# A fused attention and feed-forward kernel: the first four tiles' q and k loaded in runs of 2 KB and turned by 64-row products, with the early order planned anew

## The chip, the cores and the metric

The kernel runs on one NeuronCore of a Trainium2 chip. The metric is device time in microseconds (us) of one execution; lower is better. Five engines work side by side, each through its own instructions in order: PE (TensorE, matrix products), DVE (VectorE), ACT (ScalarE), POOL (GpSimd) and SP, whose queue here only issues DMAs.

## The reference

```python
# q, k, v: 8 x 8 heads x 576 x 64, f32; w_in 512 x 2048 and w_out 2048 x 512, f64
q_c, k_c, v_c = (t.reshape(B, H, 9, 64, 64) for t in (q, k, v))     # chunks of 64 tokens
scores = matmul(q_c, k_c.transpose(0, 1, 2, 4, 3)) / 8
attn = exp(scores - max(scores)); attn = attn / (sum(attn) + 1e-9)
x = matmul(attn, v_c)  ->  4608 tokens x 512
h = x @ w_in
out = (max(h, 0) + log1p(exp(-abs(h)))) @ w_out
```

## The kernel before

A tile is 128 tokens (two chunks) with all 8 heads; there are 36. Four tiles make a block of 512 tokens, and a block goes through the two layers in 16 steps `fc`, each with 128 columns of `w_in` (G1, `gemm1`, L707, 12 products) and the matching 128 rows of `w_out` (G2, `gemm2`, L1076, 12 products). Each f32 operand is split into a high and a low part, so that three fast products stand for one exact one. The first two steps of the first block are cut: a0 and a1 are G1 of steps 0 and 1 for tiles 0 and 1 alone (12 products of 256 columns, L707), and their G2 (6 products of 512, L1076) follow; then come the same steps for tiles 2 and 3.

The weights are f64. Each of 32 units of 512 KB (16 of `w_in`, 16 of `w_out`, in turn) goes through one of three raw buffers: `w_load` (L314, L319, on SP), `w_top` (L327, ACT or POOL), `w_low` (L337, ACT), `w_add` (L342, DVE), `w_hi` (L364, ACT or POOL), `w_lo` (L368, DVE or POOL). A raw buffer is free again when its `w_top` and `w_low` are done. Tables (`TOP_ACT`, `HI_POOL`, `LO_POOL`) choose the engine.

Attention of tiles 0 to 3 is done in these steps for each tile i: loads of q, k, v (`pe_load`, L395); T, the turning of q and k from tokens on partitions to head dimensions on partitions (`pe_t`, L439); their copies out of PSUM, tq on ACT (L445) and tk on ACT or DVE (L449, table `TK`); S, the scores, 16 products of 64 x 64 (`pe_s`, L461); max (DVE, L620); sub, the subtraction of the maximum as one product (PE, L633); exp (ACT, L640); den, three DVE instructions (L645 to L647); norm (DVE or POOL, L652, table `NORM_POOL`); E, another turning (PE, L472); ec, its copy (ACT, L476); V, 16 products (PE, L487); xh (ACT, L680) and xl (DVE, L686), the two parts of x, which G1 reads. Behind a G1 stand softplus (ACT, L715), its high part (ACT, L719) and its low part (g_lo, DVE or POOL, L723), which G2 reads. Tiles 4 and on are turned on DVE instead (STREAM_TRANSPOSE, L547 and others) and their products stand between the G1 and G2 as bursts (L560, L665).

The order on every engine is fixed when the kernel is built. A planner (`Plan`) holds every step as a task with an engine, a cost, needs, buffers and an urgency `urg`. It plays the program through and gives each free engine the ready task with the lowest `urg`. Where it sees PE without work before 90 us it puts products of the identity there as fillers: `keep_warm` (L421) before many PE tasks, `keep_busy` (L416) before V of tile 2 and before a1. In the kernel before, the urgencies of the early tasks come from `ATT_AT`, `LOAD_AT`, `DECODE_AT` and formulas; the first loads on SP are q and k of tiles 0, 1, 3 and 2, one `w_in` unit, then the four v.

```python
    def pe_load(eng, i, src, n):                       # 1024 runs of 256 bytes
        dst = hd(slot(i, n))
        for p0, rows, b, s0 in rows_of(i):
            eng.dma_start(dst[p0 : p0 + rows], src[b, :, s0 : s0 + rows, :].rearrange("h s d -> s h d"))
    ...
                nc.tensor.transpose(                   # pe_t: four for q, four for k
                    dst[:, hp * P : (hp + 1) * P], src[:, 2 * hp : 2 * hp + 2, :], ident
                )
```

Of the kernel before, what the change touches and what calls it, by code (L numbers as in the profile page):

```python
# [192 lines left out]
def chunked_attention_softplus_ffn(  # L193
# [236 lines left out]
    def pe_t(i):  # L430
        if i < 2:
            tq, tk = (po_tile(n) for n in range(2))
        else:
            tq, tk = pa_tile(), pa_tile()
        keep_warm(tq)
        for dst, n in ((tq, 0), (tk, 1)):
            src = hd(slot(i, n))
            for hp in range(HP):
                nc.tensor.transpose(  # L439
                    dst[:, hp * P : (hp + 1) * P], src[:, 2 * hp : 2 * hp + 2, :], ident  # L440
                )
        live["t", i] = tq, tk

    def pe_tq(i):
        nc.scalar.copy(slot(i, 3), live["t", i][0])  # L445

    def pe_tk(i):
        copy = nc.scalar.copy if i not in TK else nc.vector.tensor_copy
        copy(slot(i, 4), live["t", i][1])  # L449

    def pe_s(i):
        qT, kT = (slot(i, n).rearrange("p (a t) -> p a t", a=HP) for n in (3, 4))
        sc = po_tile(2 + i % 2)
        keep_warm(sc)
        for hp in range(HP):
            for c2 in range(2):
                for h2 in range(2):
                    r = slice(h2 * C, (h2 + 1) * C)
                    t = slice(c2 * C, (c2 + 1) * C)
                    col = (2 * hp + c2) * C  # L460
                    nc.tensor.matmul(  # L461
                        sc[r, col : col + C], qT[r, hp, t], kT[r, hp, t], start=hp + c2 == 0, stop=True,
                        skip_group_check=True,
                    )
        live["sc", i] = [sc.rearrange("p (a c k) -> p a c k", c=2, k=C)]
        live["e", i] = slot(i, 0).rearrange("p (a c k) -> p a c k", c=2, k=C)
# [11 lines left out]
    def pe_v(i):  # L478
        eT, vt = slot(i, 1).rearrange("p (a t) -> p a t", a=HP), hd(slot(i, 2))
        xp = [pa_tile() for _ in range(2)]  # L480
        keep_busy() if i == 2 else keep_warm(xp[0])
        for hp in range(HP):
            for h2 in range(2):
                for c2 in range(2):
                    o = slice(((h2 + c2) % 2) * C, ((h2 + c2) % 2 + 1) * C)
                    r = slice(c2 * C, (c2 + 1) * C)
                    nc.tensor.matmul(  # L487
                        xp[c2][o, hp * C : (hp + 1) * C],
                        vt[r, 2 * hp + (h2 + c2) % 2, :],
                        eT[r, hp, o],  # L490
                        start=True,
                        stop=True,
                    )
        live["xp", i] = [t[:, : HP * C].rearrange("p (c a t) -> p c a t", c=1, t=C) for t in xp]

# [604 lines left out]
    def last_half(w, j):  # L1100
# [16 lines left out]
    T0 = 30.0  # L1117
    TG = 5.2
    DECODE_AT = (-20, -2.3, -8.9, -2, -60, 1.4, 0.2, -3, 2.1, -5, 5.9, 0)
    TK = (1, 2)  # L1120
    KS = 0.2
    ATT_AT = (-52.5, 101.4, -70.6, -226.8)
    LOAD_AT = (-104.1, -66.1, -54.8, -64.2, -28.7, -42.9, -41.8, -37.3, -47.5, -9.7, -24.4, -1.0, -1.7, 22.2)
    HI_POOL = (0, 1, 2, 3, 5, 6, 7, 8, 11, 12, 13, 15, 17, 18, 19, 20, 21, 25, 31)
    WHOLE = (4, 5, 9)
    SWAP_DVE = (4, 7, 9, 10, 11, 13, 14, 15, 16, 17, 19, 20, 21, 22, 23, 24, 25, 26, 27, 28, 29, 30, 31, 32, 33, 34, 35)
    SWAP_ACT = ()
# [24 lines left out]
        ("v", 10, 0, (0, 1)), ("v", 11, 0, (0, 1)), ("q", 13, 0, (2, 3)), ("k", 13, 0, (2, 3)),  # L1152
        ("v", 16, 1, (0, 1)), ("v", 17, 1, (0, 1)), ("v", 18, 1, (2, 3)), ("v", 19, 1, (2, 3)))})
    LOAD_POOL = ()
    TOP_ACT = (1, 4, 5, 6, 7, 8, 9, 12, 13, 14, 15, 17, 18, 19, 20, 22, 24, 25, 26, 28, 30)
    LOAD_AFTER = "q0"
    LO_POOL = (2, 3, 4, 7, 9, 11, 12, 13, 14, 17, 18, 19, 22, 23, 26, 29, 31)
    NORM_POOL = (0, 3, 4, 5, 6, 8, 11, 17, 20, 21, 28, 31, 29, 33)
    GLO_POOL = (0, 3, 6, 7, 8, 10, 13, 19, 22, 26, 28)
    WO_AFTER = 1.1  # L1160
    IN_SUPER = ((0, 0, 2), (0, 0, 5), (0, 0, 7), (0, 1, 5), (1, 0, 1), (1, 0, 3), (1, 0, 5), (1, 0, 7))
# [113 lines left out]
    for i in range(FIRST_BLK):  # L1275
        d, kw = ATT_AT[i], KS
        two = 2 * i // NCH != (2 * i + 1) // NCH
        for pl, (n, src) in enumerate((("q", q), ("k", k), ("v", v))):
            plan.add(f"{n}{i}", "SP", 0.6 * (1 + two), partial(pe_load, nc.sync, i, src, pl),
                     urg=LOAD_AT[i + 4 * (pl == 2)] + 0.1 * pl, kb=310, parts=1 + two,  # L1280
                     after=[f"q{i}"] if pl else [])
        plan.add(f"T{i}", "PE", 1.0, partial(pe_t, i), [f"q{i}", f"k{i}"], urg=d,
                 take=[("po0", [f"tq{i}"]), ("po1", [f"tk{i}"])] if i < 2 else [("pa", [f"tq{i}"]), ("pa", [f"tk{i}"])])
# [541 lines left out]
```

## Time and profile before

| | us |
|---|---|
| median of 3 runs | 810.44 (810.27 to 811.56) |
| the profiled execution, its own time | 809.8 |
| its span, first to last instruction | 808.0 |
| PE busy | 797.9 (99%) |
| DVE, ACT, POOL busy | 590.0, 425.2, 362.1 |

The profile records one execution. Its span is the time from the first to the last instruction; the execution's own time is 1.8 us longer. PE counts as busy also while it works on fillers.

### The profile page before, as it was taken

Reading aid. Unit: us, or ns where it says so; the run is one execution under the profiler, and the core shown is the slowest. Engines: PE = TensorE matmul, PEld = TensorE weight load, DVE = VectorE, ACT = ScalarE, POOL = GpSimd, SP = SyncE. Lnnn points to the kernel's source line nnn. Section 1 sums busy time; section 2 is a strip of 40 time slices with the busy share of each in tenths; the row PEclk is TensorE's granted clock in tenths of the full one; section 3 lists DMA queues with packets and bytes.
Section 4 is the critical chain, followed back from the end, with each engine's and each line's share of the span. In section 5 each row is a group of like instructions: output and inputs, shape, how many; then the busy total and the mean of one; then the engine's idle time right before and its main releaser. Section 6 shows DMA issues by size and latency. Waiting matters only on the chain.

```text
span 808.0 us, 15860 instructions
## 1 busy us (share of the span) xinstructions
PE 797.9 (99%) x5668; PEld 657.0 (81%) x5668; DVE 590.0 (73%) x1085; ACT 425.2 (53%) x719; POOL 362.1 (45%) x521
## 2 busy tenths in 40 slices
PE   8999999999999999999999999999999999999997
PEld 6878778888888888888888788888888888888886
DVE  4998996387287668868875888778889864334984
ACT  3757766254344555555455365655575444445451
POOL 1557647687888451124237664344102344110213
PEclk9999999999999999999999999999999999999999
DMA  9976658765675584898997755886537867666565
GB/s 216 254 206 198 176 180 218 235 187 166 148 225 117 155 252 169 258 278 228 280 258 229 236 125 156 236 204 186 159 122 223 282 195 221 191 192 201 162 220 144
DMA packets 192574, 163.34 MB, mean 202 GB/s; under 512 B 138288, under 2 KB 160048, under 8 KB 191600
## 3 DMA queue, kind: packets, MB, share of 16 engines
q1 hardware_dynamic: 168912, 97.56, 43.3%
q0 software_dynamic: 21472, 64.51, 26.9%
q8 instruction: 45, 0.74, 0.4%
q10 hardware_dynamic: 2112, 0.26, 0.2%
q14 instruction: 33, 0.27, 0.1%
HBM read 118.49 MB, written 42.47 MB: 199 GB/s over the span
## 4 chain that ended last, share of the span: by engine, by line
PE 88%; DVE 3%; DMA 3%; SPq 2%; ACT 1%; issue 1%; POOL 0%; ACTq 0%; POOLq 0%; DVEq 0%
PE pa L832 28%; PE po L1076 23%; PE po L1012 19%; PE pa L707 13%; PE pa L665 2%; DMA raw<-in_moe_w_in_dram 2%; SPq L395 2%; PE pa L560 2%; PE po L416 1%; DMA raw<-in_moe_w_out_dram 0%; DMA eT<-ka 0%; DVE ka L547 0%; DVE qe L547 0%; DVE g_lo L723 0%; DVE wib L342 0%
## 5 line engine op out<-in xcount | busy, mean ns | idle before, releaser
L801 POOL DMA_DIRECT2D xb<-scratch x79 | 43.2, 548 | 200.4 <-PE pa L832 154.5
L832 PE MATMUL pa<-wi_hi,xb 128*128 128x512 f32 x368 | 113.3, 389 | 0.0
L832 PE MATMUL pa<-wib,xb 128*128 128x512 f32 x432 | 105.0, 389 | 0.0
L832 PEld LDWEIGHTS pa<-wib,xb 128*128 128x128 f32 x432 | 81.1, 188 | 16.9
L1076 PE MATMUL po<-late,g_hi 128*128 128x512 f32 x300 | 90.9, 392 | 0.0
L846 DVE TENSOR_TENSOR wib<-wib,pa 128x512 f32<-128x512 f32 x72 | 49.4, 686 | 55.4 <-PE pa L832 47.6
L832 PEld LDWEIGHTS pa<-wi_hi,xb 128*128 128x128 f32 x368 | 69.1, 188 | 14.3
L1054 POOL DMA_DIRECT2D out_dram<-raw x56 | 36.3, 654 | 84.6 <-DVE raw L1041 83.2
L715 ACT ACTIVATE u<-pa 128x512 f32<-128x512 f32 (+1 forms) x50 | 29.0, 580 | 83.7 <-PE pa L707 83.5
L832 PE MATMUL pa<-wi_lo,xb 128*128 128x512 f32 x184 | 71.6, 389 | 0.0
L723 DVE TENSOR_TENSOR g_lo<-u,g_hi 128x512 fp32r<-128x512 f32 (+1 forms) x39 | 29.5, 755 | 54.1 <-ACT g_hi L719 53.8
L838 ACT COPY wib<-pa 128x512 f32<-128x512 f32 x72 | 41.7, 586 | 51.8 <-PE pa L832 51.6
L1076 PEld LDWEIGHTS po<-late,g_hi 128*128 128x128 f32 x300 | 55.8, 188 | 11.8
L1076 PE MATMUL po<-wo_hi,g_hi 128*128 128x512 f32 x160 | 59.6, 395 | 0.0
L1076 PE MATMUL po<-wo_hi,g_lo 128*128 128x512 f32 x160 | 59.0, 391 | 0.0
L1076 PE MATMUL po<-wo_lo,g_hi 128*128 128x512 f32 x160 | 58.8, 390 | 0.0
L1076 PE MATMUL po<-late,g_lo 128*128 128x512 f32 x160 | 58.4, 389 | 0.0
L707 PE MATMUL pa<-xb,wib 128*128 128x512 f32 x192 | 46.6, 390 | 0.8 <-DVE wib L368 0.5
L584 DVE STREAM_TRANSPOSE eT<-qe 32x256 f32<-32x256 f32 x104 | 45.1, 434 | 1.4
L1012 PE MATMUL po<-late,xb 128*128 128x512 f32 x180 | 43.9, 389 | 0.0
L707 PEld LDWEIGHTS pa<-xb,wib 128*128 128x128 f32 x192 | 35.8, 188 | 9.2 <-DVE wib L368 0.9
L832 PEld LDWEIGHTS pa<-wi_lo,xb 128*128 128x128 f32 x184 | 34.5, 188 | 7.3
(276 smaller groups left out, 1895.0 us busy)
## 6 DMA issues: line engine op xcount, KB each, us to landing
xb<-scratch POOLq DMA_DIRECT2D x48, 512.0 KB, 4.0
xb<-images SPq DMA_DIRECT2D x32, 512.0 KB, 4.7
raw<-in_moe_w_in_dram SPq DMA_DIRECT2D x16, 512.0 KB, 5.6
raw<-in_moe_w_out_dram SPq DMA_DIRECT2D x16, 512.0 KB, 4.5
scratch<-ends SPq DMA_DIRECT2D x16, 512.0 KB, 2.9
xb<-scratch POOLq DMA_DIRECT2D x7, 1024.0 KB, 6.6
xb<-scratch POOLq DMA_DIRECT2D x8, 768.0 KB, 7.5
late<-images SPq DMA_DIRECT2D x22, 256.0 KB, 4.2
```

What stands on the lines that cost most here:

```text
L395: eng.dma_start(dst[p0 : p0 + rows], src[b, :, s0 : s0 + rows, :].rearrange("h s d -> s h d"))
L584: nc.vector.transpose(live["eT", i][d : d + BL, tb], e[s : s + BL, kb])
L707: nc.tensor.matmul(ph, wt[:, c, :], x[:, ts_, c, :], start=(n == 0), stop=(n == 3 * KC - 1))
L715: nc.scalar.activation(w["u"], w["ph"], AF.Softplus)
L723: (nc.gpsimd if pool else nc.vector).tensor_tensor(w["lo"], w["u"], w["hi"].bitcast(F32), op=ALU.subtract)
L801: on("ring").dma_start(t[:, n * MT : (n + len(ks)) * MT], src[:, ks[0] * MT : (ks[-1] + 1) * MT])
L832: nc.tensor.matmul(w["bank"][BANK[k]], wts[:, q, c, :], x[:, c, :], start=k in OPENS and c + n == 0, stop=c == 1 and n == 2, skip_group_ch ...
L838: nc.scalar.copy(tmp_of(n), w["bank"][2 * (n == 2)])
L846: nc.vector.tensor_tensor(to, a, b, op=ALU.add)
L1012: nc.tensor.matmul(live["acc", ACC[k]][ct], image_part(n, k, j, q)[:, ct * P : (ct + 1) * P], g, start=k < 3 and j == 0 and i < len(cts), ...
L1054: eng.dma_start(out[r0 : r0 + MT, c0 : c0 + BL].rearrange("(b t) d -> t b d", t=BL), t.rearrange("t (b d) -> t b d", d=BL))
L1076: nc.tensor.matmul(pos[w["m"]][t], terms[n][0][:, j * P : (j + 1) * P], terms[n][1], start=(w["first"] and n == 0), stop=n == 2 and (w["la ...
```

## The change

q and k of tiles 0 to 3 are read as `h x (j d)`: head h and 16 groups x of 8 consecutive tokens j give the 128 partitions, and each partition holds 8 tokens of one head, 2 KB in one run. There are now 128 runs instead of 1024. v is loaded as before. A partition so holds (head, group), and a 512-wide row holds (token in the group, head dimension). T takes, for each of the 8 tokens j and each half a of the partitions (four heads), one 64 x 64 product with the identity: 16 products for q and 16 for k instead of four transposes of 128 x 128 each. The result has its columns in the order j, head, group, so tq and tk read PSUM with a stride (`in_order`) and write in order. S and V take their heads from other places; their products are as many and as large as before.

The rest is order. A table `START` gives new urgencies to all early tasks (some 300 of them, up to the last weight unit), and five tables move steps between engines: `TK` (tk on DVE: tiles 1 and 2 before, tile 3 now), `HI_POOL` (19 units before, 18 now), `TOP_ACT` (21 before, 19 now), `LO_POOL` (17 and 17), `NORM_POOL` (14 and 14).

```diff
     def pe_load(eng, i, src, n):
+        if n < 2:
+            (_, _, b, s0), = rows_of(i)
+            eng.dma_start(
+                slot(i, n), src[b, :, s0 : s0 + P, :].rearrange("h (x j) d -> h x (j d)", j=H)
+            )
+            return
         dst = hd(slot(i, n))
...
         for dst, n in ((tq, 0), (tk, 1)):
-            src = hd(slot(i, n))
-            for hp in range(HP):
-                nc.tensor.transpose(
-                    dst[:, hp * P : (hp + 1) * P], src[:, 2 * hp : 2 * hp + 2, :], ident
-                )
+            src = slot(i, n)
+            for j in range(H):
+                for a in range(2):
+                    r, col = slice(a * C, (a + 1) * C), slice(j * C, (j + 1) * C)
+                    nc.tensor.matmul(dst[r, col], src[r, col], ident[r, r], start=True, stop=True, skip_group_check=True)
...
+    def in_order(t):
+        return t.rearrange("p (j x) -> p x j", j=H)
+
     def pe_tq(i):
-        nc.scalar.copy(slot(i, 3), live["t", i][0])
+        nc.scalar.copy(slot(i, 3).rearrange("p (x j) -> p x j", j=H), in_order(live["t", i][0]))
...
+    START = dict(
+        q0=-55.2, k0=-55.15, q1=-42.45, k1=-42.6, q2=-55, T0=-51.9, k2=-42.55, tq0=63.85, tk0=59.32, S0=-51.9, w_top0=59.22,
...
-    TK = (1, 2)
+    TK = (3,)
...
+    for name, urg in START.items():
+        plan.tasks[name]["urg"] = urg
     plan.emit()
```

What the new order is, at three places. The first is PE at its start (`late0` and `late1` are q and k of tile 0, `late5` and `late6` those of tile 1, `xa` those of tile 3; `po` and `pa` are PSUM). Before:

```order
L439 MATMUL po0_150<-ident_92,late0_131 128x128 x4
L439 MATMUL po1_151<-ident_92,late1_132 128x128 x4
L421 MATMUL po2_179<-ident_92 128x128 x3
L461 MATMUL po2_179<-late4_135,late3_134 64x64 x16
L439 MATMUL po0_200<-ident_92,late5_138 128x128 x4
L439 MATMUL po1_201<-ident_92,late6_139 128x128 x4
L633 MATMUL po2_179<-mx_210,minus_97 128x512
```

And now:

```order
L447 MATMUL po0_152<-ident_92,late0_131 64x64 x16
L447 MATMUL po1_153<-ident_92,late1_132 64x64 x16
L447 MATMUL pa_196<-ident_92,xa_122 64x64 x16
L447 MATMUL pa_197<-ident_92,xa_122 64x64 x16
L470 MATMUL po2_236<-late4_135,late3_134 64x64 x16
L470 MATMUL po3_256<-ka_140,qe_139 64x64 x16
L639 MATMUL po2_236<-mx_275,minus_97 128x512
```

T of tile 3 now follows T of tile 0 at once, ahead of both S; behind the rows shown come sub of tile 3, T of tiles 2 and 1, S of both, E of tile 0, and sub of both.

The second place is PE around a0 and a1. Before, where a0 is ahead of the first row and the first G2 follows a1:

```order
L487 MATMUL pa<-xa,eT 64x64 x16
L416 MATMUL po_479<-ident 128x128 x10
L487 MATMUL pa<-late_169,late_170 64x64 x16
L416 MATMUL po_523<-ident 128x128 x12
L707 MATMUL pa<-xb,wi_hi 128x256 x4
L707 MATMUL pa<-xb,wi_lo 128x256 x4
```

And now:

```order
L497 MATMUL pa<-xa,eT 64x64 x16
L481 MATMUL po_509<-ident,late_230 128x128 x4
L497 MATMUL pa<-late_144,late_145 64x64 x16
L497 MATMUL pa<-late_231,late_232 64x64 x16
L427 MATMUL pa<-ident 128x128
L713 MATMUL pa<-xb,wi_hi 128x256 x4
L713 MATMUL pa<-xb,wi_lo 128x256 x4
L713 MATMUL pa<-xb,wi_hi 128x256 x8
```

All four V (tiles 0, 3, 2 and 1) stand ahead of a0, a1 follows a0 directly, and the 22 fillers of L416 are gone; behind a1 stand three fillers and then the first G2, that of a0.

The third place is DVE ahead of the low part of a0's softplus (the last row of each; `xb` is x, `wib` the weight units, `q` and `k` those of tile 4). Before:

```order
L686 TENSOR_TENSOR xb_354<-pa_379,xb_353 128x256
L686 TENSOR_TENSOR xb_354<-pa_380,xb_353 128x256
L547 STREAM_TRANSPOSE qe_442<-q_348 32x8x32 x4
L342 ISA wib1_103<-wib1_103,ends_124 128x1024
L368 TENSOR_TENSOR wi_lo_101<-wib0_102,wi_hi_100 128x512
L686 TENSOR_TENSOR xb_354<-pa_450,xb_353 128x256
L686 TENSOR_TENSOR xb_354<-pa_451,xb_353 128x256
L723 TENSOR_TENSOR g_lo_551<-u_468,g_hi_514 128x256
```

And now:

```order
L692 TENSOR_TENSOR xb_481<-pa_518,xb_480 128x256
L692 TENSOR_TENSOR xb_481<-pa_519,xb_480 128x256
L368 TENSOR_TENSOR wo_lo1_109<-wib1_103,wo_hi1_108 128x512
L342 ISA wib0_102<-wib0_102,ends_124 128x1024
L692 TENSOR_TENSOR xb_481<-pa_548,xb_480 128x256
L692 TENSOR_TENSOR xb_481<-pa_549,xb_480 128x256
L342 ISA wib1_103<-wib1_103,ends_124 128x1024
L553 STREAM_TRANSPOSE ka_599<-k_506 32x8x32 x4
L553 STREAM_TRANSPOSE qe_623<-q_450 32x8x32 x4
L729 TENSOR_TENSOR g_lo_632<-u_619,g_hi_629 128x256
```

In both, eight transposes of tile 4 stand ahead of that low part; now they follow xl of the last tile, with one more unit's sum (L342) ahead of them. Up to that low part DVE has six sums and three low parts of weights in the changed order, and four and two in the order before.

## Rows read from the trace of the kernel before

**Rows 1.** The page: the span, and busy time by engine.

```profile
span 808.0 us, 15860 instructions
PE 797.9 (99%) x5668; PEld 657.0 (81%) x5668; DVE 590.0 (73%) x1085; ACT 425.2 (53%) x719; POOL 362.1 (45%) x521
```

**Rows 2.** PE in order of time: start, us, line, xcount [idle before <-releaser].

```profile
26.77 0.69 PE L487 MATMUL pa<-xa,eT 64*64 64x64 f32 x32
27.39 2.50 PE L416 MATMUL po<-ident 128*128 128x128 f32 x20
...
30.45 2.94 PE L416 MATMUL po<-ident 128*128 128x128 f32 x24
33.15 0.72 PE L707 MATMUL pa<-xb,wi_hi 128*128 128x256 f32 x4
...
34.67 0.63 PE L1076 MATMUL po<-wo_hi,g_hi 128*128 128x512 f32 x2
```

**Rows 3.** The same view, the three waits of PE from 34 us to 798 us.

```profile
58.68 1.16 PE L707 MATMUL pa<-xb,wi_hi 128*128 128x512 f32 x4 [0.20 <-DVE qe L627]
...
83.67 2.97 PE L707 MATMUL pa<-xb,wib 128*128 128x512 f32 x12 [0.35 <-DVE qe L627]
...
112.50 2.11 PE L707 MATMUL pa<-xb,wib 128*128 128x512 f32 x8 [0.48 <-DVE wib L368]
```

**Rows 4.** The same view, PE up to 20 us.

```profile
1.35 3.60 PE L421 MATMUL po<-ident 128*128 128x128 f32 x16 [1.35 <-POOL ident masks.py:199]
4.79 1.15 PE L439 MATMUL po<-ident,late 128*128 128x128 f32 x8
...
12.94 1.02 PE L633 MATMUL po<-mx,minus 128*128 128x512 f32 x2
13.97 1.15 PE L461 MATMUL po<-late,late 64*64 64x64 f32 x32
15.05 0.66 PE L472 MATMUL po<-ident,late 128*128 128x128 f32 x4
...
19.18 0.69 PE L487 MATMUL pa<-late,late 64*64 64x64 f32 x32 [1.33 <-DMA late<-in_v_dram]
```

**Rows 5.** DMA, 5 to 11 us: packets; then GB/s from 0 to 45 us in 40 slices.

```profile
DMA packets 5214, 1.31 MB, mean 219 GB/s; under 512 B 5214, under 2 KB 5214, under 8 KB 5214
...
GB/s 0 45 257 234 227 221 217 218 218 223 279 324 231 221 165 229 243 343 358 379 290 165 101 290 321 231 305 294 327 156 319 296 224 26 211 254 117 375 200 167
```

**Rows 6.** DVE in order of time.

```profile
16.05 0.68 DVE L645 TENSOR_REDUCE den<-late 128x8 f32<-128x512 f32 x1
...
17.09 0.64 DVE L620 TENSOR_REDUCE mx<-po 128x8 f32<-128x512 f32 x1
...
23.22 2.14 DVE L342 CUSTOM_DVE_ANT_0 wib<-wib,ends 128x1024 uint16<-128x1024 uint16 x2
...
27.74 0.69 DVE L342 CUSTOM_DVE_ANT_0 wib<-wib,ends 128x1024 uint16<-128x1024 uint16 x1
28.35 0.68 DVE L368 TENSOR_TENSOR wi_lo<-wib,wi_hi 128x512 fp32r<-128x512 f32 x1
29.05 1.79 DVE L547 STREAM_TRANSPOSE qe<-q 32x256 f32<-32x256 f32 x4
30.87 1.42 DVE L686 TENSOR_TENSOR xb<-pa,xb 128x256 fp32r<-128x256 f32 x4
32.21 0.41 DVE L723 TENSOR_TENSOR g_lo<-u,g_hi 128x256 fp32r<-128x256 f32 x1
```

**Rows 7.** ACT in order of time.

```profile
10.80 0.58 ACT L449 COPY ka<-pa 128x512 f32<-128x512 f32 x1
...
23.23 0.79 ACT L327 CAST ends<-raw 128x512 f16<-128x512 bf16 x1 [0.61 <-DMA raw<-in_moe_w_in_dram]
```

**Rows 8.** POOL in order of time.

```profile
11.68 1.04 POOL L652 TENSOR_TENSOR late<-late,den 128x512 f32<-128x512 f32 x1 [9.76 <-DVE den L647]
```

More of the change, by code (lines that the diff above doesn't have):

```diff
@@ L436, in pe_t @@
         for dst, n in ((tq, 0), (tk, 1)):
-            src = hd(slot(i, n))
-            for hp in range(HP):
-                nc.tensor.transpose(
-                    dst[:, hp * P : (hp + 1) * P], src[:, 2 * hp : 2 * hp + 2, :], ident
-                )
+            src = slot(i, n)
[3 more added lines that the diff above has]
+                    nc.tensor.matmul(dst[r, col], src[r, col], ident[r, r], start=True, stop=True, skip_group_check=True)
         live["t", i] = tq, tk
+    def in_order(t):
+        return t.rearrange("p (j x) -> p x j", j=H)
     def pe_tq(i):
-        nc.scalar.copy(slot(i, 3), live["t", i][0])
+        nc.scalar.copy(slot(i, 3).rearrange("p (x j) -> p x j", j=H), in_order(live["t", i][0]))
     def pe_tk(i):
         copy = nc.scalar.copy if i not in TK else nc.vector.tensor_copy
-        copy(slot(i, 4), live["t", i][1])
+        copy(slot(i, 4).rearrange("p (x j) -> p x j", j=H), in_order(live["t", i][1]))
     def pe_s(i):
-        qT, kT = (slot(i, n).rearrange("p (a t) -> p a t", a=HP) for n in (3, 4))
+        qT, kT = (slot(i, n).rearrange("p (h t) -> p h t", h=HP) for n in (3, 4))
         sc = po_tile(2 + i % 2)
         keep_warm(sc)
-        for hp in range(HP):
+        for hl in range(HP):
             for c2 in range(2):
-                for h2 in range(2):
-                    r = slice(h2 * C, (h2 + 1) * C)
+                for a in range(2):
+                    r = slice(a * C, (a + 1) * C)
                     t = slice(c2 * C, (c2 + 1) * C)
-                    col = (2 * hp + c2) * C
+                    col = (2 * hl + c2) * C
                     nc.tensor.matmul(
-                        sc[r, col : col + C], qT[r, hp, t], kT[r, hp, t], start=hp + c2 == 0, stop=True,
+                        sc[r, col : col + C], qT[r, hl, t], kT[r, hl, t], start=hl + c2 == 0, stop=True,
                         skip_group_check=True,
@@ L482, in pe_v @@
         for hp in range(HP):
-            for h2 in range(2):
+            for n in range(2):
                 for c2 in range(2):
-                    o = slice(((h2 + c2) % 2) * C, ((h2 + c2) % 2 + 1) * C)
-                    r = slice(c2 * C, (c2 + 1) * C)
+                    h2 = (n + c2) % 2
+                    h = 2 * hp + h2
+                    o, r, t = (slice(m * C, (m + 1) * C) for m in (h2, c2, h // HP))
                     nc.tensor.matmul(
[L488 to L492, printed above, removed]
+                        xp[c2][o, hp * C : (hp + 1) * C], vt[r, h, :], eT[r, h % HP, t], start=True, stop=True
                     )
@@ L1123, in chunked_attention_softplus_ffn @@
     LOAD_AT = (-104.1, -66.1, -54.8, -64.2, -28.7, -42.9, -41.8, -37.3, -47.5, -9.7, -24.4, -1.0, -1.7, 22.2)
-    HI_POOL = (0, 1, 2, 3, 5, 6, 7, 8, 11, 12, 13, 15, 17, 18, 19, 20, 21, 25, 31)
+    HI_POOL = (0, 1, 2, 4, 5, 6, 10, 11, 12, 13, 15, 17, 18, 19, 20, 21, 25, 31)
     WHOLE = (4, 5, 9)
@@ L1154, in chunked_attention_softplus_ffn @@
     LOAD_POOL = ()
-    TOP_ACT = (1, 4, 5, 6, 7, 8, 9, 12, 13, 14, 15, 17, 18, 19, 20, 22, 24, 25, 26, 28, 30)
+    TOP_ACT = (1, 2, 6, 8, 9, 12, 13, 14, 15, 17, 18, 19, 20, 22, 24, 25, 26, 28, 30)
     LOAD_AFTER = "q0"
-    LO_POOL = (2, 3, 4, 7, 9, 11, 12, 13, 14, 17, 18, 19, 22, 23, 26, 29, 31)
-    NORM_POOL = (0, 3, 4, 5, 6, 8, 11, 17, 20, 21, 28, 31, 29, 33)
+    LO_POOL = (2, 3, 6, 8, 10, 11, 12, 13, 14, 17, 18, 19, 22, 23, 26, 29, 31)
+    NORM_POOL = (2, 3, 4, 5, 6, 8, 11, 17, 20, 21, 28, 29, 31, 33)
     GLO_POOL = (0, 3, 6, 7, 8, 10, 13, 19, 22, 26, 28)
@@ L1279, in chunked_attention_softplus_ffn @@
             plan.add(f"{n}{i}", "SP", 0.6 * (1 + two), partial(pe_load, nc.sync, i, src, pl),
-                     urg=LOAD_AT[i + 4 * (pl == 2)] + 0.1 * pl, kb=310, parts=1 + two,
+                     urg=LOAD_AT[i + 4 * (pl == 2)] + 0.1 * pl, kb=310 if pl == 2 else 230, parts=1 + two,
                      after=[f"q{i}"] if pl else [])
```

34 lines of the change are left out of this document (added).

## The prediction

> **What bounds the kernel now.** I read the page first: PE is busy for 797.9 us of a span of 808.0 [rows 1]. Fillers count as busy there, so the question is from when on PE's work is all useful and unbroken. PE in order of time answers it: 44 filler products stand between 27.4 and 33.4 us, a1 starts at 33.15, and the first product of the second layer (the first G2, that of a0) at 34.67 [rows 2]. From there to 800 us the same view has three waits of PE, 0.20, 0.35 and 0.48 us, each ended by DVE [rows 3]. So the end of the kernel is the start of that first G2, plus a fixed list of products, plus 1.03 us of waits. A change of the early part can pay in two ways only: the first G2 starts earlier, or those waits go. Nothing beyond 1.03 us can come from weights that are ready sooner.
>
> **The loads.** Eight loads of 256 KB go from 1024 runs of 256 bytes to 128 runs of 2 KB. While runs of 256 bytes alone were moved, all were under 512 bytes and the rate was 219 GB/s; the best slices with long runs show 343 to 379 GB/s [rows 5]. A load so falls from 1.20 us (262 KB by 219) to about 0.71 (by 370), eight of them by 3.9 us. Both ends: nothing, if the run length isn't what limits, and 4.0 us at 379. On the path it is worth little. The fillers held PE until T of tile 0 began at 4.79 [rows 4]; one filler of eight goes, 1/8 of 3.60, so T can start at about 4.3. After that PE is the later one, as the next part shows. The weights behind these loads do come some 4 us sooner, which helps the waits of [rows 3].
>
> **The turning.** T was 8 transposes in 1.15 us, and the next PE work followed after about 1.1 [rows 4]. It becomes 32 products of 64 x 64 in two of the array's four quarters (rows and columns are cut by the same half). The nearest rows are S, 16 such products in the same two quarters: it starts at 13.97 and the next at 15.05, so 1.08 us [rows 4]. T so takes 2.15. Ends: V runs 16 products of that size over all four quarters in 0.69 [rows 4], so 1.4 for T is the low end, the old 1.1 the lowest; twice the 1.15 that S shows, 2.3, the high one. I take 2.15, since S has T's shape and its quarters. Four tiles: 4 x 1.05 = 4.2 us more PE work ahead of the first G2. The Trainium skill (TensorEngine Tiling (Array Packing), Restrictions and Gotchas) speaks against this change: with the columns cut, the transpose mode for f32 isn't to be had. No run here shows the rule itself; that S, by ordinary products, has twice as many PE records as calls, and the transposes one each, fits it. With the transposes' old price kept, the sum below would be 4.2 us less.
>
> **tq and tk.** Their copies read PSUM with a stride. A plain copy takes 0.58; a strided cast on ACT 0.79 [rows 7]. I take 0.58, the same shape and type, and keep 0.2 more for each, of which two stand on the path.
>
> **The new order, step by step** (us from the span's start; each step begins where its last input or its engine is free). T of tiles 0 and 3: 4.3 to 8.6. S of both: 10.8. sub of both, 1.0 each [rows 4]: 12.8. T of tiles 2 and 1: 17.1. S of tile 2: 18.2. S of tile 1 waits for two copies behind the last T, 0.55 each: 18.3 to 19.4. E of tile 0, 0.6 [rows 4], and sub of tile 2: 21.05. exp of tile 2, 0.6: 21.7. den, 1.04 for its three instructions from 16.05 to 17.09 [rows 6]: 22.8. norm of tile 2 is on POOL, 1.04 [rows 8]: 23.9. E of tile 2, V of tile 3, E of tile 1 and V of tile 2, 0.6 each on PE: 26.4. xh of tile 2, behind the copy of tile 1's E on ACT: 27.3. From here DVE is full: xl of tile 2, 0.7; a low part, 0.68; a sum, 0.65; xl of tile 1, 0.7; a sum, 0.65; eight transposes of tile 4, twice 1.79; g_lo, 0.41 [rows 6]: 27.3 + 7.4 = 34.7. a0 and a1 are done by about 32, and PE then has little. With 0.2 from DVE to PE the first G2 starts at **34.9**, against 34.67. No v is late in this: all loads up to the last v are 5.2 MB, by about 20 us at the rates above, ahead of its V.
>
> So the fillers that go (2.50 and 2.94 us) and the loads bring nothing: dearer turns and a DVE queue take their place. What DVE has gained is work: at its g_lo of a0 it has two sums and a low part more behind it than before, and one tk copy less to do. That is 1.9 us ahead, and the first two of the three waits of [rows 3] were at products that waited for DVE's subtractions, the third for a low part of a weight on DVE. I let 0.20 and 0.48 go and keep 0.35, whose burst is ordered much as before.
>
> **What moves between engines.** Two w_top from ACT to POOL, one w_hi from POOL to ACT, one tk from DVE to ACT: POOL has 0.9 us more, ACT 0.4 less, DVE 0.7 less. I cost these at nothing: POOL is busy for 45% [rows 1]. If that cover is gone, it shows on DVE, where two sums beside POOL's work took 2.14 us [rows 6] instead of 1.3.
>
> **The sum.** +0.2 for the first G2, -0.7 for the waits: -0.5. Against the profiled execution's 809.8 that is 809.3; the median of the runs shown stands 0.6 above it, so **809.9**. Ends: the first G2 4.2 us earlier with all waits gone gives 805.4; 0.4 for the copies, two hits of 0.85 on DVE and no wait gone give 812.7. A measurement of this kernel can tell about 0.2%, 1.6 us, from no change.
>
> **Rival 1, turns that cost little: faster.** Everything up to the last V hangs on PE, so a cheaper T goes through whole. At the transposes' price the time is 809.9 - 4.2 = 805.7; half way, 807.8. For it: V shows that 64 x 64 products can run at 0.69 for 16. Against it: V uses four quarters, T two. The Trainium skill (TensorEngine Tiling (Array Packing), Tiling Modes) counts four such tiles that work independently; by that the price of V would hold only for products over all four, and the rows of S and V agree. A shorter DVE queue ahead of g_lo would do the same in part. It decides from a first G2 ahead of 33.8. I give it 0.32.
>
> **Rival 2, DVE held up by POOL: slower.** Place: DVE from 20 to 35 us. There are eight DVE instructions of weights and norm ahead of g_lo, and POOL now has more of the same. In the row of 23.22 POOL's norm ran beside two sums, and they took 0.85 longer [rows 6]. Two such hits, the dearer copies (0.4) and no wait gone: 809.9 + 1.7 + 0.4 + 0.7 = 812.7. For it: in the new order g_lo is the last of a full queue, so each hit goes through whole. Against it: xl waits for ACT in between, which takes up the first. It decides from a first G2 behind 36.5. I give it 0.15.
>
> **Rival 3, the clock: slower.** With 22 filler calls gone, PE idles for most of the time from 32 to 34.9. The first fillers took 0.225 each, at the lower clock of 1.2 GHz; the later ones 2.50 for 20, so 0.125, at 2.4 [rows 2, 4]. The clock rose by about 4.8 us, some 3.4 us after PE's first product [rows 4]. If it falls in the gap, PE works at half rate for as long again and loses 1.7: 811.6. Against it: a wait of 1.33 us with thin work around it left the products behind it at their full rate [rows 4]. The Trainium skill (TensorE: Matmul & The Clock Gate, HAM oscillation) names gaps between groups of products as what throttles the clock again, and a busy start as what pays once more; no row before shows it in mid-run. I give it 0.07.
>
> **How the numbers follow.** The forecast has 0.46; its own range is 808.9 to 812.0, the part of the ends that a measurement can't tell from no change. Faster by over 0.2% is rival 1: 0.32. Slower is rivals 2 and 3: 0.22. The range reaches down to 806.2, between rival 1's two times, and up to 812.2, between those of rivals 2 and 3; about 1 in 10 is left out at each side.
>
> **What would show it.** T as 64 records in 2.1 us, with the next PE work right behind; T of the last tile ending near 17; the q and k loads' issues on SP at about half their time; the first G2 at 34 to 36, with the g_lo of a0 right ahead of it on DVE behind eight transposes; PE's waits behind it under 0.7 us in sum; the granted clock at full throughout. I am wrong in size if T takes 1.1 to 1.5 or the first G2 is at 33 or earlier, in sign if it is behind 36.5, and in mechanism if PE's waits behind it grow.

## The result, and the profile after

The changed kernel takes 815.88 us (median of 6 runs, 815.47 to 817.5) against 810.71 (6 runs, 810.12 to 811.72): 1.0067 times as long, 95% interval 1.0054 to 1.008. It is slower by 5.2 us where no change was forecast, outside the range. The profiled execution took 815.57 us, its span is 813.8, 5.8 more than before.

The page of the changed kernel (as [rows 1]):

```profile
span 813.8 us, 16206 instructions
PE 800.0 (98%) x5846; PEld 659.5 (81%) x5846; DVE 588.3 (72%) x1084; ACT 424.7 (52%) x719; POOL 362.5 (45%) x522
```

PE of the changed kernel in order of time (start, us, line, xcount, [idle before <-releaser]), as [rows 2 to 4]. L447 is T, L470 S, L497 V, L713 a0 and a1, L1082 the first G2:

```profile
4.82 1.15 PE L447 MATMUL po<-ident,late 64*64 64x64 f32 x32
6.40 1.15 PE L447 MATMUL po<-ident,late 64*64 64x64 f32 x32 [0.44 <-DMA late<-in_k_dram]
7.78 1.15 PE L447 MATMUL pa<-ident,xa 64*64 64x64 f32 x32 [0.23 <-DMA xa<-in_q_dram]
9.41 1.15 PE L447 MATMUL pa<-ident,xa 64*64 64x64 f32 x32 [0.49 <-DMA xa<-in_k_dram]
10.39 1.10 PE L470 MATMUL po<-late,late 64*64 64x64 f32 x32
...
16.30 1.15 PE L447 MATMUL pa<-ident,late 64*64 64x64 f32 x32 [0.71 <-DMA late<-in_k_dram]
18.71 3.50 PE L447 MATMUL po<-ident,late 64*64 64x64 f32 x64 [1.27 <-DMA late<-in_q_dram]
22.04 1.11 PE L470 MATMUL po<-late,late 64*64 64x64 f32 x32
...
35.36 1.09 PE L713 MATMUL pa<-xb,wi_hi 128*128 128x256 f32 x4 [0.32 <-ACT xb L686]
...
40.41 0.71 PE L1082 MATMUL po<-wo_hi,g_hi 128*128 128x512 f32 x2
...
41.43 0.62 PE L1082 MATMUL po<-wo_hi,g_lo 128*128 128x512 f32 x2
...
117.39 2.12 PE L713 MATMUL pa<-xb,wib 128*128 128x512 f32 x8 [0.60 <-DVE wib L368]
```

Half a turn costs 0.98 us where work follows at once (9.41 to 10.39), within 0.1 of the forecast. But PE waits for q and k five times, 3.14 us in sum, where before the list of its waits has none for them; and T of tile 1 takes 3.50 for 64 records. The first G2 starts at 40.41 instead of 34.67: 5.74 us, the whole loss. Two waits follow it, 0.60 and 0.21, against three of 1.03 in sum.

DVE of the changed kernel, the low part of a0 (g_lo):

```profile
40.52 0.42 DVE L729 TENSOR_TENSOR g_lo<-u,g_hi 128x256 fp32r<-128x256 f32 x1
```

The same kernel by stretches (us, busy time and instructions of each engine, granted clock, DMA share, GB/s), and behind it the first stretch of the kernel before:

```profile
2.50:6.50 4.00, 3.45 (x45) 3.02 (x45) 0.00 (x0) 0.00 (x0) 0.00 (x0) 1.00 0.50 169
18.50:22.00 3.50, 3.29 (x64) 3.32 (x65) 0.59 (x1) 0.07 (x1) 0.05 (x1) 0.52 0.95 285
35.50:39.00 3.50, 3.50 (x18) 3.50 (x18) 3.44 (x9) 2.98 (x5) 2.40 (x3) 0.51 0.93 285
```

```profile
2.50:6.50 4.00, 4.00 (x27) 3.78 (x25) 0.00 (x0) 1.08 (x2) 0.00 (x0) 1.00 1.28 240
```

While almost only runs of 2 KB are moved, the DMA share is 0.50 and the rate is 169 GB/s instead of 240: longer runs, and slower. And the granted clock is 0.52 and 0.51, the lower level of 1.2 GHz, under T of tile 1 and under a0 and a1; in the kernel before the clock's row has 1.00 throughout. PE had idled several times ahead of both.

SP of the changed kernel in order of time (DMA issues: start, us):

```profile
2.24 0.60 SPq L395 DMA_DIRECT2D xa<-in_q_dram  x1
...
4.66 2.02 SPq L314 DMA_DIRECT2D raw<-in_moe_w_in_dram  x1
6.72 1.39 SPq L395 DMA_DIRECT2D late<-in_k_dram  x1
...
9.41 1.64 SPq L395 DMA_DIRECT2D late<-in_k_dram  x1
```

An issue is down to 0.60, but the four from 4.66 on take 1.2 to 2.0 us; no run here shows what holds SP. The last k is issued at 9.41; before, all eight were out by 8.5.

### The profile page after: what moved, and what is told of

Read it like the earlier page. It is cut to its first block, busy times and chain, and to the rows that moved or that the text cites. A ratio compares the mean times of both kernels' runs of the same rounds, so it can differ in the third digit from the quotient of the medians.

```text
span 813.8 us, 16206 instructions
## 1 busy us (share of the span) xinstructions
PE 800.0 (98%) x5846; PEld 659.5 (81%) x5846; DVE 588.3 (72%) x1084; ACT 424.7 (52%) x719; POOL 362.5 (45%) x522
## 4 chain that ended last, share of the span: by engine, by line
PE 87%; DMA 4%; POOL 2%; DVE 2%; ACT 2%; issue 1%; SPq 1%; DVEq 0%; POOLq 0%; ACTq 0%
PE pa L838 27%; PE po L1082 21%; PE po L1018 19%; PE pa L713 15%; PE pa L671 2%; PE pa L566 2%; DMA late<-in_q_dram 1%; DMA xb<-scratch 1%; POOL raw L536 1%; DMA k<-in_k_dram 1%; SPq L395 1%; DMA raw<-in_k_dram 1%; PE po L447 0%; DMA raw<-in_moe_w_out_dram 0%; DVE eT L602 0%
## 5 line engine op out<-in xcount | busy, mean ns | idle before, releaser
L1082 PE MATMUL po<-late,g_hi 128*128 128x512 f32 x300 | 91.2, 392 | 0.0
L1082 PEld LDWEIGHTS po<-late,g_hi 128*128 128x128 f32 x300 | 55.8, 188 | 12.2 <-DVE late L368 0.4
L1082 PE MATMUL po<-wo_hi,g_hi 128*128 128x512 f32 x160 | 59.7, 395 | 0.0
L1082 PE MATMUL po<-wo_hi,g_lo 128*128 128x512 f32 x160 | 59.0, 391 | 0.0
L1082 PE MATMUL po<-wo_lo,g_hi 128*128 128x512 f32 x160 | 58.8, 390 | 0.0
L1082 PE MATMUL po<-late,g_lo 128*128 128x512 f32 x160 | 58.4, 389 | 0.0
L713 PE MATMUL pa<-xb,wib 128*128 128x512 f32 x192 | 46.4, 390 | 0.6 <-DVE wib L368 0.6
L713 PEld LDWEIGHTS pa<-xb,wib 128*128 128x128 f32 x192 | 36.0, 188 | 8.5 <-DVE wib L368 1.0
```

Of the source, the lines that this page charges most:

```text
L713: nc.tensor.matmul(ph, wt[:, c, :], x[:, ts_, c, :], start=(n == 0), stop=(n == 3 * KC - 1))
L1082: nc.tensor.matmul(pos[w["m"]][t], terms[n][0][:, j * P : (j + 1) * P], terms[n][1], start=(w["first"] and n == 0), stop=n == 2 and (w["la ...
```

## The experiments

The Trainium skill (DMA: Bandwidth & Descriptors, How many engines (k)) says that a DMA from a hardware queue is spread over the largest number of engines, 16 at most, that divides the slowest dimension of both access patterns. The changed loads have heads, 8, as the slowest dimension of the source. That rule gave theory A. Times in the table are in us, "first G2" is its start, and "records" are those that PE shows for one product of T. All times below are medians beside runs of the kernel before on the same chip (810.3 to 810.6; 810.71 beside the change).

| run | loads | turning | order | us | ratio (95%) | first G2 |
|---|---|---|---|---|---|---|
| change | heads first | two records | new | 815.88 | 1.0067 (1.0054 to 1.008) | 40.41 |
| e1 | groups first | two records | new | 816.72 | 1.0079 (1.0066 to 1.0092) | 40.20 |
| e6 | heads first | one record | new | 816.83 | 1.0077 (1.0065 to 1.0089) | 38.23 |
| e5 | groups first | one record | new | 811.11 | 1.0006 (0.9996 to 1.0016) | 34.38 |
| e3 | as before | as before | new | 811.09 | 1.0013 (1.0001 to 1.0024) | 34.86 |
| e2 | heads first | two records | old | 816.87 | 1.0079 (1.0063 to 1.0095) | 38.79 |
| e7 | groups first | two records | old | 816.91 | 1.0074 (1.0061 to 1.0087) | 41.39 |
| e8 | groups first | one record | old | 811.83 | 1.0024 (1.0008 to 1.004) | 36.07 |

### Which part costs: e1 to e4

**e1_groups_first**

```diff
-                slot(i, n), src[b, :, s0 : s0 + P, :].rearrange("h (x j) d -> h x (j d)", j=H)
+                slot(i, n), src[b, :, s0 : s0 + P, :].rearrange("h (x j) d -> x h (j d)", j=H)
```

> The changed kernel with one line other: each q and k load walks the group of eight tokens first and the head second, so the same 128 runs of 2 KB of a load go to other partitions, with a slowest dimension of 16 instead of 8. Nothing else moves. This changes the computation: a partition holds another head and group than the turning takes it for, so times alone count. Theory A (a load with a slowest dimension of 8 is moved by half of the DMA engines, and the first G2 is late because q and k are): the DMA share from 2.5 to 6.5 us goes from 0.50 to about 1, PE's five waits for q and k (3.1 us in sum) go, the fall of the clock at 18.5 us goes too; first G2 at 36 to 37.5 us instead of 40.4; 811 to 813 us. Theory B (runs of 2 KB are no faster whatever walks them, or PE's dearer turns and the new order set the time): the share stays near 0.5 and the time at 815 to 816.5; or the loads land sooner and the first G2 still stands behind 39.5.

816.72 us. The stretch from 2.5 to 6.5 us:

```profile
2.50:6.50 4.00, 4.00 (x45) 3.78 (x45) 0.00 (x0) 0.00 (x0) 0.00 (x0) 1.00 1.02 268
```

PE of the same run:

```profile
1.35 3.35 PE L427 MATMUL po<-ident 128*128 128x128 f32 x14 [1.35 <-POOL ident masks.py:199]
4.63 3.40 PE L447 MATMUL po<-ident,late 64*64 64x64 f32 x64
7.87 2.03 PE L447 MATMUL pa<-ident,xa 64*64 64x64 f32 x64
9.74 1.10 PE L470 MATMUL po<-late,late 64*64 64x64 f32 x32
10.79 1.15 PE L470 MATMUL po<-ka,qe 64*64 64x64 f32 x32
11.87 1.98 PE L639 MATMUL po<-mx,minus 128*128 128x512 f32 x4
13.78 0.56 PE L447 MATMUL pa<-ident,late 64*64 64x64 f32 x12
15.72 1.67 PE L447 MATMUL pa<-ident,late 64*64 64x64 f32 x51 [1.37 <-issue]
...
19.16 0.45 PE L470 MATMUL po<-late,late 64*64 64x64 f32 x10
22.75 1.78 PE L470 MATMUL po<-late,late 64*64 64x64 f32 x53 [3.15 <-issue]
...
40.20 0.71 PE L1082 MATMUL po<-wo_hi,g_hi 128*128 128x512 f32 x2
...
473.30 0.69 PE L566 MATMUL pa<-ka,qe 64*64 64x64 f32 x32 [1.68 <-DVE ka L543]
```

The first half of theory A is shown: one dimension moved doubles the DMA share, the rate goes from 169 to 268 GB/s and all five waits for q and k are gone. So the Trainium skill's rule agrees with the row. The second half fell: not a microsecond was won. In the middle of T of tile 2 and of S of tile 2 PE stands still for 1.37 and 3.15 us, and "issue" says that nothing in the profile ended these waits. They eat up all that the loads gained. The last row is a wait of which the change has 0.21; most of the 1.6 us by which this run ends later than its first G2 alone would make it.

**e2_loads_alone**: the kernel before with the changed `pe_load`, `pe_t`, `pe_tq`, `pe_tk`, `pe_s` and `pe_v`, and nothing else.

> The kernel before with the changed loads, turning, copies, S and V alone: its tables, its urgencies, so its order on every engine and its fillers. Theory A (the loads on half of the engines and the dearer turns make it slower, whatever the order): PE waits for q and k here too; the first G2 is at 37.5 to 40 us instead of 34.7; 813.5 to 816 us. Theory B (the new order is what costs, the loads and turns are hidden): first G2 at 34.7 to 36, 810.5 to 812.

816.87 us, just above theory A's range. PE of that run:

```profile
17.17 1.15 PE L447 MATMUL pa<-ident,late 64*64 64x64 f32 x32 [0.54 <-DMA late<-in_k_dram]
...
38.79 0.63 PE L1082 MATMUL po<-wo_hi,g_hi 128*128 128x512 f32 x2
```

The first G2 is 4.12 us later. The forecast's price for four turns was 4 x 1.05 = 4.2, and here, with the 44 fillers, the granted clock is 1.00 throughout. From each T to PE's next work, waits left out, the four T take 8.8 us against 4.2 before, 4.6 more: the term is right. That the first G2 comes so close to it is in part luck: PE starts T of tile 0 0.27 later and waits 0.54 for a k, and the wait of 1.33 for v [rows 4] is gone. The remaining 1.9 us of the profiled execution come later, in single waits (0.7 for a softplus's high part on ACT).

**e3_order_alone**: the changed kernel with the functions of `pe_load`, `pe_t`, `pe_tq`, `pe_tk`, `pe_s` and `pe_v` from the kernel before.

> The changed kernel with the loads, turning, copies, S and V of the kernel before: runs of 256 bytes, eight transposes for a tile; the new urgencies and tables, so the new order on every engine. Theory A (the order is as good as the old one or better; loads and turns cost the time): first G2 at 33 to 36 us, 808.5 to 811.5. Theory B (the order costs by itself, by its DVE queue, or by PE idling where the 22 fillers stood, so that the clock falls): first G2 behind 37, 813 to 816, with a fall of the clock in the early part.

811.09 us. PE of that run:

```profile
16.32 1.08 PE L439 MATMUL po<-ident,late 128*128 128x128 f32 x4 [1.38 <-DMA late<-in_k_dram]
...
34.86 0.73 PE L1076 MATMUL po<-wo_hi,g_hi 128*128 128x512 f32 x2
...
36.78 0.73 PE L1076 MATMUL po<-wo_hi,g_lo 128*128 128x512 f32 x2 [0.72 <-DVE g_lo L723]
```

The order costs next to nothing by itself (1.0013): theory A. Yet PE waits five times for q and k here too, 3.13 us in sum, as much as in the change: in the new order PE is ahead of the old loads as well. What is left of the loss, over 4 us, belongs to loads and turns. The forecast's DVE queue is there too: the low part of a0 comes last, 0.72 late.

**e4_fillers**

```diff
+            keep_up(dst, {(1, 0): 10, (2, 1): 4}.get((i, n), 0))      # pe_t, ahead of q or k
...
+        keep_up(xp[0], 10 if i == 1 else 0)                           # pe_v
```

> The changed kernel with 24 more products of the identity on PE: 10 ahead of T of tile 1, 4 ahead of the turning of k of tile 2, 10 ahead of V of tile 1, where PE idled for 1.27, 0.71 and 1.30 us. If the two falls of the clock (3.4 us at half rate each, at 18.5 and 35.5) cost time on the path, each costs up to 1.7: with both gone 812 to 813.5, with one gone 813.5 to 814.5. If they are hidden behind ACT and DVE, 815 to 816. In both the loads still land late and the first waits for q and k stay.

818.42 us (ratio 1.0103, 1.009 to 1.0116): a miss on every account. The granted clock stayed at 1.00, but the fillers took longer than the waits they stood in: T of tile 1 began at 20.72 instead of 18.71, and those ahead of V of tile 1 began only at 34.20, because the PSUM tile that I gave them was V's own and not free before. So this run does not price the clock.

### Two covers, one over the other: e5 to e8

After e1 there were two suspects, the late loads and something that stops PE in the turns. T on the upper 16 bits as bf16 makes one record of a product instead of two.

```diff
+    def upper(t):
+        return t.bitcast(BF16).rearrange("p (f t) -> p f t", t=2)[:, :, 1]
...
-                    nc.tensor.matmul(dst[r, col], src[r, col], ident[r, r], start=True, stop=True, skip_group_check=True)
+                    nc.tensor.matmul(dst[r, col], upper(src)[r, col], upper(ident)[r, r], start=True, stop=True, skip_group_check=True)
```

**e5_groups_onepass**: this and e1's line. **e6_onepass**: this alone.

> The kernel with the group ahead of the head in the loads, with T's 32 products for a tile on the upper 16 bits of their f32 operands, as bf16: one record for a call instead of two. The turned q and k are rounded and, as in the run before, from other heads, so times alone count. The order on every engine is that of the changed kernel. Theory C (with the loads in time, PE ran out of instructions: the two waits that nothing in the profile ended, 1.37 and 3.15 us, each end 1.5 us behind a 16 KB transfer of the instruction queue, and T has 64 records for a tile where the transposes had 8): half the records of T cost half the time and half the instructions; both waits go or shrink to under 1 us in sum; first G2 at 33.5 to 36.5 us instead of 40.2, 808.5 to 812. Theory D (what stands behind the turns sets the start of the first G2, not T and not its instructions): first G2 at 38.5 to 40.5, 814 to 816.5.

> The changed kernel as it is, its loads with heads first, with T's products on the upper 16 bits as bf16, one record for a call. q and k are rounded by it. If the late loads (half of the DMA engines) hold the path, cheaper turns only lengthen PE's waits for q and k, from 3.1 us in sum to 5 or more, and the first G2 stays at 38.5 to 40.4: 813.5 to 815.9. If the turns' own time is what counts, the first G2 is 2 to 4 us earlier: 811.5 to 813.5.

811.11 and 816.83 us. PE of e6, which has the loads of the change:

```profile
9.03 0.64 PE L450 MATMUL pa<-ident,xa 64*64 64x64 bf16 x16 [1.94 <-DMA xa<-in_q_dram]
...
20.93 0.44 PE L450 MATMUL po<-ident,late 64*64 64x64 bf16 x16 [1.49 <-DMA late<-in_k_dram]
```

And of e5:

```profile
15.94 0.44 PE L450 MATMUL po<-ident,late 64*64 64x64 bf16 x16 [1.42 <-DMA late<-in_k_dram]
```

Cheaper turns alone bring no time: the waits for q and k grow to 6.6 us in sum. The first G2 does come 2.2 earlier, at 38.23, but single waits behind it (0.72 for g_lo, 0.77, 0.79) take that back, so e6 misses the times of both its cases. Better loads alone (e1) bring nothing either. Both together (e5) bring 5 us, back to the kernel before. Late loads and turns lay over the same time, and each was enough for the loss. As e5 halves T's time and its instructions alike, it doesn't tell which of the two counted.

In e3, e5 and e6, which have the same order, PE waits for the k of tile 1, so the rows show when it lands: at 16.32 with the old loads, at 20.93 with heads first, at 15.94 with groups first. Heads first cost the last load 4.6 us; with groups first, runs of 2 KB won only 0.4.

**e7_old_order_groups** and **e8_old_order_groups_onepass**: the same two edits on e2.

> The old order with the changed loads and turns, and the group ahead of the head in the loads, so that a load is spread over twice as many DMA engines; output from other heads, times alone count. If the late loads made the old order with the new loads 6 us slower: first G2 back from 38.8 to 35 to 36.5 us, 811 to 812.5. If T's own 1.05 us more for a tile did, or PE's instructions: first G2 at 38 to 40, 814 to 818; by theory C with waits of PE that nothing in the profile ends, over 1 us each, behind 12 us.

> The old order, the group ahead of the head in the loads, and T's products on the upper 16 bits as bf16 (rounded q and k of other heads; times alone count). This has the early loads at their full rate and a turn of about the transposes' price, so it shows what runs of 2 KB are worth by themselves. By theory C: first G2 at 33.5 to 34.7 us, no waits that nothing ends, 808.5 to 810.5. If loads that land sooner collide with what follows (v, weights, instructions): first G2 behind 35, 811 or more.

816.91 and 811.83 us. PE of e7, and behind it one row of e8:

```profile
12.09 1.38 PE L447 MATMUL pa<-ident,xa 64*64 64x64 f32 x38
15.73 1.65 PE L447 MATMUL pa<-ident,xa 64*64 64x64 f32 x25 [2.27 <-issue]
...
41.39 0.63 PE L1082 MATMUL po<-wo_hi,g_hi 128*128 128x512 f32 x2
```

```profile
15.67 1.03 PE L473 MATMUL po<-late,late 64*64 64x64 f32 x28 [1.25 <-issue]
```

In the old order better loads make the first G2 later than in e2 by 2.6 us, by a wait that nothing ends; its time fits the second case, its first G2 is later than that had it. e8 fell to its second case: even with half the records of T PE waits so once, for 1.25 us until 15.67, and the first G2 is at 36.07. Three programs that stand at different places (T of tile 2, T of tile 3, a late S) all go on at 15.7: no step of the kernel ends these waits. What they share is the count. In e1 PE has issued 14 fillers, 64 + 64 products of T, 32 + 32 of S, 4 of sub and 12 of T when it stops: 222 records. The rows of e7 and e8 add up to 222 as well, and so do those of e9 and of e12 (0.19 us ahead of 15.43) below.

### What stops PE: e9

**e9_loads_first**: e1, with the issue of two loads deferred.

```diff
+    held = []
+    for name in ("v2", "load0"):
+        plan.tasks[name]["fn"] = partial(held.append, plan.tasks[name]["fn"])
+    k1 = plan.tasks["k1"]["fn"]
+    plan.tasks["k1"]["fn"] = lambda: [fn() for fn in [k1] + held]
     plan.emit()
```

> The kernel with the group ahead of the head in the loads (e1), whose v of tile 2 and first w_in unit are issued on SP behind the eight q and k instead of between them; every other engine has the same instructions in the same order. In e1 PE stood still twice with nothing in the profile to end it, until 1.5 us after a 16 KB transfer on the instruction queue had ended. Theory C (PE waits for its instructions): wherever these transfers now fall, PE goes on 1.4 to 1.6 us after each end; if they stand in line behind the loads, the first starts before 12 us instead of 12.95 and the wait of 1.37 gets shorter, with v and weights later; 814 to 817. Rival (something else stops PE there): the waits end at times that have nothing to do with these transfers.

813.9 us (1.004, 1.0027 to 1.0053). PE of e9:

```profile
13.60 1.67 PE L447 MATMUL pa<-ident,late 64*64 64x64 f32 x51 [0.58 <-issue]
...
19.81 1.78 PE L470 MATMUL po<-late,late 64*64 64x64 f32 x53 [1.79 <-issue]
...
36.13 0.73 PE L1082 MATMUL po<-wo_hi,g_hi 128*128 128x512 f32 x2
```

The DMA view of e1 by short stretches, 12.9 to 13.0, 12.9 to 14.3, 19.9 to 20.0 and 19.9 to 21.3 us (queue, packets, MB, share of 16 engines' time); from 0 to 12.9 the instruction queue has no packet. The last row is that queue in the whole run of the change:

```profile
q8 instruction: 1, 0.02, 78.7%
...
q8 instruction: 1, 0.02, 5.6%
...
q8 instruction: 1, 0.02, 80.5%
...
q8 instruction: 1, 0.02, 5.8%
...
q8 instruction: 46, 0.75, 0.4%
```

And of e9, 10.7 to 12.2 and 17.0 to 18.4 us (each stretch begins with the packet):

```profile
q8 instruction: 1, 0.02, 5.8%
...
q8 instruction: 1, 0.02, 5.7%
```

A share of 5.6% of 16 engines over 1.4 us is 1.25 us: one packet from 12.9 on, done by about 14.2. PE goes on at 15.72. The second lasts 1.30 us from 19.9, done by 21.25; PE goes on at 22.75. In e9 the packets end at about 12.1 and 18.3, and PE goes on at 13.60 and 19.81. Four times about 1.5 us after the end; and where two loads, 0.79 MB, are issued behind the others, packets and restarts come earlier alike, the first by 2.1 us and the second by 2.9. So theory C holds: PE waited for its own instructions. Between the two stops of e1 lie 51 + 1 + 1 + 62 + 1 + 1 + 10 = 127 product records, with as many weight loads 254 instructions. The Trainium skill (Runtime: NRT & Kernel Launch, Instruction fetch mechanics) says that instructions come in blocks of 16 KiB, 256 instructions, and that crossing a block's end is mostly hidden. The size agrees with the count, with the packet of 0.02 MB and with the number of packets: PE's 5846 products and as many weight loads are 45.7 times 256. That it is hidden does not agree here, with 4.5 us of waits in e1.

When a packet was asked for is not recorded, so that it stood in line behind loads is argued, not shown. e9 alone can't show it: PE was ahead of e1 there by 1.3 us before the first stop (S of tile 0 at 8.41 instead of 9.74, as T of tile 0 took 2.08 instead of 3.40), and the second packet follows the first restart. What speaks for it: the first packet starts at 12.7 to 13.9 us in the nine programs whose early loads use all engines and keep their place, but at 11.05 in the change, at 10.81 in e2 and at 11.05 in e4, whose q and k keep half of them busy; and PE is behind e1 in the change (S of tile 0 at 10.39). e6, with the loads of the change, lies between at 12.06; PE is later still there (S of tile 0 at 11.34).

T of tile 0 is also a warning about single traces: it took 1.15 us in the kernel before and 1.69 in e11, which runs the same program up to there. A first G2 is read from one execution each time.

### The clock, and the start of the old order: e10 to e12

**e10_order_fillers** (e3 with 21 products of the identity in `pe_t`) and **e12_onepass_fillers** (e5 with 41, in `pe_t`, `pe_e` and `pe_v`; those of `pe_v` on another PSUM tile than in e4):

```diff
+            keep_up(dst, {(3, 0): 3, (3, 1): 4, (1, 0): 4, (1, 1): 10}.get((i, n), 0))      # e10
...
+            keep_up(dst, {(3, 0): 7, (3, 1): 5, (1, 1): 10}.get((i, n), 0))                 # e12
+        keep_up(tp, {3: 5, 2: 6}.get(i, 0))                                                 # e12, pe_e
+        if i == 1:
+            keep_up(po_tile(2), 8)                                                          # e12, pe_v
```

> The new order with the loads, turning, S and V of the kernel before (e3), and 21 more products of the identity on PE where it waited for loads: 3 and 4 ahead of the turning of q and k of tile 3, 4 and 10 ahead of those of tile 1. In e3 the clock was at half rate from 16 to 19.3 us, under T and S of tile 1 and S of tile 2. If that costs time on the path: full rate throughout, the last early S ends at 18.5 to 19 instead of 20.2, the products of the first G2 that need its low part 0.8 to 1.6 us earlier than 36.78, 809.3 to 810.4. If the clock is hidden behind DVE and ACT: 811 as before.

> The run with group-first loads and T on the upper 16 bits (e5), and 41 more products of the identity where its PE waited: 7 and 5 ahead of the turning of q and k of tile 3, 10 ahead of that of k of tile 1, 5 ahead of E of tile 3, 6 of E of tile 2, 8 of V of tile 1. q and k are rounded and of other heads; times alone count. In e5 the clock was at half rate for 3.4 us twice before the first G2, under S of tiles 0 and 3 and under a0 and a1. With the clock kept up: first G2 at 32 to 33.5 instead of 34.4, 808.5 to 810: what the early part is worth with loads at full rate, cheap turns and the new order. If the first G2 is held by its softplus on ACT and DVE: 34 or later, 810.5 to 811.5.

e10 took 811.71 us (1.0016, 1.0005 to 1.0026), e3 811.09: no difference that these runs can tell. The granted clock was 1.00 throughout and the products with the low part of a0 came 0.66 earlier (36.12 instead of 36.78); that is less than I gave it, and the time falls to the second case. e12 took 812.51 (1.0025, 1.0015 to 1.0036): the fillers kept the clock up but overran the waits, and the first G2 came at 36.37 instead of 34.38: a miss. What the clock's two falls cost the changed kernel is not settled as a whole: on PE, T of tile 1 took 3.50 instead of 2.08 in e4, and from the start of a0 to the end of a1 4.5 us instead of 3.1 in e3, but no run removes them alone. The second can be bounded from the rows of the change. Its g_lo starts at 40.52, at the end of an unbroken DVE queue, and the products with it at 41.43; in e3, where PE waited for g_lo, they start 0.48 behind it (36.30, 36.78). So an earlier end of a0 and a1 could have brought 0.4 us at most.

**e11_before_fewer**

```diff
-        for _ in range(int(IDLE_FILL * (plan.idle - 0.3) / 0.112)):
+        for _ in range(n):                # keep_busy(7) ahead of V, keep_busy(5) ahead of a1
```

> The kernel before with fewer fillers in its two late groups: 7 instead of 10 ahead of V of tile 2, 5 instead of 12 ahead of a1 (L416); nothing else. By the trace of before V's buffers are free at about 29.0 and x of tile 2 is there by 31.2 (its low part by 32.3), while the fillers end at 29.8 and 33.15. If the end is the start of the first G2 plus a fixed list: first G2 at 33.0 to 33.8 instead of 34.67, 809.0 to 810.0. If weights or DVE are next: PE's waits behind the first G2 grow from 1.03 by what the start gains, 810.5. If the clock falls: 811 to 812.5.

808.93 us against 810.37: ratio 0.9987 (0.9978 to 0.9996, 12 runs), a small gain, just clear of none, and ahead of both kernels. PE of that run:

```profile
31.41 0.71 PE L707 MATMUL pa<-xb,wi_hi 128*128 128x256 f32 x4 [0.31 <-DVE xb L686]
...
32.92 0.63 PE L1076 MATMUL po<-wo_hi,g_hi 128*128 128x512 f32 x2
```

The fillers of the kernel before were themselves late: a1 now waits 0.31 for its input and starts 1.74 earlier. The last part of PE's work starts 1.1 earlier (801.25 instead of 802.37).

## Why the prediction was wrong

- **The end is the first G2 plus a fixed list.** Right for the change: the first G2 is 5.74 later, the last part of PE starts 5.78 later (808.15 against 802.37). As a rule it is good to some 3 us: e1 lost 1.6 more on the way, e2 1.8, e6 2.9, and e11 gave back 0.6 of its 1.75.
- **The turning, 2.15 for a tile.** Right: 0.98 for half a turn where work follows at once, and 8.8 for e2's four against 8.6. With it rival 1 fell.
- **The loads, 1.20 to 0.71 each, "After that PE is the later one".** This step failed. I read the 219 GB/s of [rows 5] as a matter of run length alone and did not ask how many engines a load would use. The row showed 169 GB/s at a share of 0.50; e1 showed 268 at 1.02 with the same runs, not the 370 I took. With heads first the loads were slower than before, not faster: 240 GB/s fell to 169, and the k of tile 1 landed 4.6 us later than with the old loads in the same order (e6, e3). And PE was not the later one: it waited five times for q and k, 3.14 us, and even with the old loads 3.13 (e3).
- **The new order, S of tiles 2 and 1 done by 19.4.** They were done by 24.5. The 5.1 between, by the rows: T of tile 0 0.5 later, waits for q and k 3.14, T of tile 1 at the lower clock 1.35, one wait of 0.23, together 5.2. From there to the first G2 I had 15.5 us, and it took 15.9, but that is luck. I let the first G2 wait for g_lo, and only its third pair of products needs it (e3: first G2 at 34.86, that pair at 36.78). In the change PE was busy from 35.36 with a0 and a1, at the lower clock, and fillers until the first G2; g_lo came in time for its pair.
- **Costed at nothing: PE's instructions.** T has 64 records for a tile instead of 8. I priced their time and not their fetch. In the change it is hidden: the first packet ended at 12.2 and the 222nd record falls into T of tile 2, behind 14.44. With loads in time (e1, e7) it is what stands behind them.
- **The waits of 0.20 and 0.48 go.** 0.20 and 0.35 went; the one at the weight's low part grew to 0.60. About 0.2 of the 0.7 came.
- **Rival 2** is not needed: e3 has the same DVE queue and 1.0013. **Rival 3** named a fall of the clock, but in a gap behind a1, and there was none; it fell twice earlier, and only the price of the second fall is bounded. (I read the lower level at the start from the fillers' 0.225 us; the profile's row of the clock has 1.00 there.) The slower side's real mechanism, loads on half of the engines, was no rival of mine at all.

## What to carry to other kernels

The length of its runs alone doesn't give a load's rate (169 or 268 GB/s here, with the same runs): look at the DMA share while it runs alone, and at the slowest dimension of its access pattern. An operation cut into many small products is paid in instructions too: look for waits of PE that nothing ends, beside packets of the instruction queue. And where removing a cause brings nothing, remove the next one with it before it is acquitted: e1 and e6 each looked like proof that the other part was all that mattered.

## What the runs showed of the hardware that I had not expected

PE ran out of instructions while the loads were moved: stops of 1.37, 3.15, 2.27 and 1.25 us, each over about 1.5 us after a packet of 16 KB had ended, the first always behind PE's 222nd product record. Loads of 256 KB in 128 runs of 2 KB went at 169 or at 268 GB/s, by which of two dimensions comes first. And a PE that mostly turns small products between waits of 0.2 to 1.3 us fell to the lower clock (18.5 to 21.9 us in the change), while with fillers in such gaps it stayed up (e4, e10, e12).
